# Order of the GpSimd work in a fused attention and routing kernel: where kept sums are weighed, where weight sums stand, and how group ends are cut

## The chip, the cores and the metric

The kernel runs on one core of one Trainium2 chip. The metric is device time in microseconds (us). A core has a matrix engine (PE, with its weight loads as PEld), a vector engine (DVE), a scalar engine (ACT), a general engine (POOL, GpSimd) and a sync engine (SP). Each takes its instructions strictly in the order of its own queue, and waits at the head of the queue until what an instruction needs is there. Almost all DMAs of this kernel are issued from SP's queue.

## What is computed

A polynomial-sketch attention gives x of 4352 rows and 128 columns; eight experts with a hidden layer of 1024 then work on x, each expert's output is multiplied by a routing weight per row (from a Sinkhorn iteration), and the eight are added:

```python
logits = x @ w_gate
P = np.exp(logits - logits.max())
for _ in range(8):
    P /= P.sum(1, keepdims=True) + 1e-09
    P /= P.sum(0, keepdims=True) + 1e-09
    P *= N / E
for e in range(E):
    h = np.maximum(x @ w1[e], 0.0)
    out += P[:, e:e + 1] * (h @ w2[e])
```

All is float32. The routing weights are positive, so x may be multiplied by the weight ahead of the first product: `relu(P x w1) w2` is `P (relu(x w1) w2)`. The kernel does so for most of the work.

## The kernel before

x is kept transposed, features on the partitions and 4352 rows of x as columns (`xT`). The expert work is cut into **groups** of columns (line 536 on) and, within a group, into **items**, one per expert. A step of an item is a first product (line 788: two halves of the output), its relu on ACT (line 792), additions on DVE that prepare a fast matrix multiplication in the manner of Strassen (two tiles at a time: lines 807 to 810; three tiles at a time: lines 841 and 861), and eight steps later the second products (line 931), which add up in four PSUM banks over all experts of the group. The second products use sums and differences of blocks of w2, which POOL makes once per expert (`sums_of_two`, lines 186 to 189; `sums_of_four`, line 225, ten instructions), stores to DRAM and later loads again (lines 182, 213).

Items 0 to 6 are unweighted: they run while the routing weights are still being computed (expert 0 on all columns, expert 1 on the first 1280), and their results stay in SBUF as **kept** sums. Items 7 to 46 are weighted. They form five groups of 3 x 256 columns (experts 1 to 7, or 2 to 7 in the group that starts at column 512), whose items have two blocks of eight steps, and a last group of 2 x 256 columns (experts 2 to 7), whose items have four blocks of four steps. For a weighted item, `prepare_x` loads the expert's routing weights, the same row on all partitions, from the DRAM tensor `pT` into a tile `xe` (line 562), and POOL multiplies x into it (line 574). Tiles `xe` and the weight tiles have two buffers each, so a load for an item waits until the item before the last is through with its buffer.

The kept sums must be weighed too before they are added at the group's end: `weigh_kept` loads weights into a tile `pb` (line 562; one buffer) and POOL multiplies them into the kept sums (line 585), and adds two such products where experts 0 and 1 were both kept (line 587). It is called when the second item of a weighted group starts.

At a group's end `part_of_twenty` combines the four banks in some 20 small operations, handed to DVE and ACT one per step (`at_leisure`), then adds the kept sums to all 768 columns at once, and `put` turns the result (line 598, DVE) and stores it with DMAs from SP (line 754): one per block of 32 features, twice as many where the columns cross one of the four batches of 34 blocks of 32 columns.

What sets the order: a planner (the Tile framework) places the instructions of every engine and queue. During the attention, and until the first weighted items, DVE and PE have the order in which the code names them. POOL and SP are free throughout, and in the rest of the weighted part all engines are: the planner takes an instruction when it estimates that its inputs and its buffer are ready, with program order as the rank. So an instruction that is named late can stand early in a queue. `keep_in_program_order(i)` ties `i` behind the instruction named just before it on the same engine or queue; it orders the issue and doesn't wait for the other to finish. Before, only four memsets have it (lines 465, 467).

The work is named in `steps`: at the start of item j it prepares weights and x of items j and j + 1, and then, in the group's second item, weighs the kept sums.

Of the kernel before, what the change touches and what calls it, by code (L numbers as in the profile page):

```python
# [10 lines left out]
F32 = mybir.dt.float32  # L11
U32 = mybir.dt.uint32
Act = mybir.ActivationFunctionType
Alu = mybir.AluOpType
# [36 lines left out]
def kernel(  # L51
# [12 lines left out]
    nc = tc.nc  # L64
    P = nc.NUM_PARTITIONS
# [63 lines left out]
    pT = dram.tile([E, N], F32, name="pT")  # L129
# [3 lines left out]
    for i in range(2):  # L133
        t = consts.tile([P, 2, 2, 2, D], F32, name=f"kvz{i}")
# [4 lines left out]
    for i in range(2):  # L139
        t = wk.tile([P, H + 1, NT + 1, D], F32, name=f"v{i}", bufs=1)  # L140
# [3 lines left out]
    loaded, pools = {}, []  # L144
# [64 lines left out]
    def sums_of_four(e, w2):  # L209

        ws = pools[0].tile([P, len(FORMS), FO // 4, H2], F32, tag="ws4", name="ws4")
        if e in stored_four:
            nc.sync.dma_start(out=ws, in_=stored_four[e])
            return ws

        def blocks(bs):
            b = w2[:, bs[0][1]::4, H2 * bs[0][0]:H2 * (bs[0][0] + 1)].unsqueeze(1)
            if len(bs) == 1:
                return b
            step = (bs[1][1] - bs[0][1]) * DM + (bs[1][0] - bs[0][0]) * H2  # L220
            return AP(tensor=b.tensor, offset=b.offset, ap=[b.ap[0], [step, 2], *b.ap[2:]])

        c = 0
        for ns, x, y, off in FOURS:
            nc.gpsimd.tensor_tensor(ws[:, c:c + len(ns)], blocks(x), blocks(y), op=Alu.subtract if off else Alu.add)  # L225
            c += len(ns)
        stored_four[e] = dram.tile([P, len(FORMS), FO // 4, H2], F32, name=f"ws4{e}")
        nc.sync.dma_start(out=stored_four[e], in_=ws)
        return ws
# [294 lines left out]
    NT3 = 256  # L524
# [33 lines left out]
                loaded_w[j] = *loaded_w[j][0:2], sums_of_four(e, loaded_w[j][1])  # L558

    def weights_of(e, lo, n, tag):  # L560
        pb = pools[0].tile([P, 3 * NT3], F32, tag=tag, name=tag, bufs=2 if tag == "xe" else 1)[:, 0:n]
        nc.sync.dma_start(out=pb, in_=pT[e:e + 1, lo:lo + n].to_broadcast([P, n]))
        return pb

    def prepare_x(j):
        g, e = items[j]
        lo, n, t, es, weighted = groups[g]
        x = xT[:, lo:lo + t * n]
        if not weighted:
            sources[j] = x  # L570
            return
        xe = weights_of(e, lo, t * n, "xe")
        for sl in (slice(0, 512), slice(512, 768)) if j == first_weighted else (slice(0, t * n),):
            nc.gpsimd.tensor_tensor(xe[:, sl], x[:, sl], xe[:, sl], op=Alu.mult)  # L574
        sources[j] = xe

    first_weighted = next(j for j, (g, e) in enumerate(items) if g == PLAIN)
# [1 line left out]
    def weigh_kept(g):  # L579

        lo, n, t, es, _ = groups[g]
        ys = []
        for e in range(es[0]):
            ys.append(kept[e][:, lo:lo + n * t])
            nc.gpsimd.tensor_tensor(ys[e], ys[e], weights_of(e, lo, n * t, "pb"), op=Alu.mult)  # L585
        for y in ys[1:]:
            nc.gpsimd.tensor_tensor(ys[0], ys[0], y, op=Alu.add)

    lower, upper = slice(0, H2), slice(H2, P)

    def at_leisure(do):

        soon.append(lambda: later.append(do))

    def put(y, lo, n, queues):
        b0, nb = lo // 32, n // 32
        yt = pools[0].tile([P, 3 * NT3 // 32, 32], F32, tag="yt", name="yt")[:, 0:nb, :]
        nc.vector.transpose(out=yt.rearrange("p b d -> p (b d)"), in_=y)
        store(yt, b0, b0 + nb, queues)

# [92 lines left out]
    def part_of_twenty(g, k):  # L693


        lo = groups[g][0]
        own = parts.setdefault(g, {})
        own[k] = room("zwmf"[k]).rearrange("p (s n) -> p s n", s=2)
        nc.scalar.copy(own[k].rearrange("p s n -> p (s n)"), sums[g][k])

        def do(out, a, b, off=False):
            at_leisure(lambda: nc.vector.tensor_tensor(out, a, b, op=Alu.subtract if off else Alu.add))  # L702

        if k == 0:
            own["y"] = pools[0].tile([P, 3, NT3], F32, tag="y", name="y")
            do(own["y"][:, 0], own[0][:, 0], own[0][:, 1])
        y = own["y"]
        if k == 1:
            do(y[:, 1], own[1][:, 0], own[0][:, 0], True)
        elif k == 2:  # L710
            do(y[upper, 2], own[2][upper, 0], own[0][upper, 0], True)
            do(y[lower, 2], own[2][lower, 0], own[0][lower, 1], True)
            do(y[lower, 2], y[lower, 2], own[2][lower, 1], True)
            do(y[lower, 1], y[lower, 1], own[1][lower, 1], True)
        elif k == 3:
            e0, e1, e2, e3 = (own[i] for i in range(4))
            t, c = (room(a).rearrange("p (s n) -> p s n", s=2) for a in "rx")
            d = e0[:, 1]

            def across(out, a):  # L720
                at_leisure(lambda: nc.scalar.copy(out, a))

            do(t[:, 0], e2[:, 1], e3[:, 0])
            do(t[:, 1], e1[:, 1], e3[:, 1], True)
            do(d[upper], t[upper, 1], e3[upper, 0], True)
            across(c[lower, 1], t[upper, 0])
            across(c[upper, 1], e3[lower, 0])
            do(t[upper, 1], d[upper], e2[upper, 1], True)
            do(t[lower, 1], t[lower, 0], t[lower, 1])
            across(d[lower], d[upper])  # L730
            across(c[lower, 0], t[upper, 1])
            across(c[upper, 0], t[lower, 1])
            do(e0[upper, 0], e1[upper, 1], e3[upper, 0], True)
            do(e0[upper, 0], e2[upper, 1], e0[upper, 0], True)
            do(y[upper, 1], y[upper, 1], e0[upper, 0])
            do(c[lower, 1], e3[lower, 0], c[lower, 1], True)
            do(y[:, 1], y[:, 1], c[:, 1], True)
            do(y[:, 0], y[:, 0], t[:, 1])
            do(y[:, 0], y[:, 0], c[:, 0])
            do(y[upper, 2], y[upper, 2], t[upper, 1], True)  # L740
            do(y[lower, 2], y[lower, 2], d[lower], True)
            flat = y.rearrange("p t n -> p (t n)")
            do(flat, flat, kept[0][:, lo:lo + 3 * NT3])
            at_leisure(lambda: put(flat, lo, 3 * NT3, (nc.sync,)))

    ends = (nc.scalar, nc.sync, nc.gpsimd, nc.scalar), (nc.sync, nc.scalar, nc.gpsimd, nc.sync)

# [190 lines left out]
    def steps():  # L938

        todo, sums_at, t = {}, {}, 0  # L940
        for k in range(len(blocks) + 2):
            if k == len(blocks):
                for i, ps in enumerate(last_products(k - 2)):
                    todo[t + i] = ps
            if k < len(blocks):
                j, q = blocks[k]
                g, e = items[j]
                lo, n, tiles, es, weighted = groups[g]
                if q == 0:
                    for i in (j, j + 1, j + 2 if j + 2 < first_weighted else j):  # L950
                        if i < len(items) and i not in loaded_w and (pools or i < first_weighted):
                            prepare_w(i)
                        if i < len(items) and i not in sources and (pools or i < first_weighted):
                            prepare_x(i)
                    if weighted and e == es[1]:
                        weigh_kept(g)
                m, step, sums_ = (four if tiles == 3 else two)(k)
                products = (twenty if tiles == 3 else seven)
            for c in range(m if k < len(blocks) else 4):
                if k < len(blocks):  # L960
                    step(c)
                for do in sums_at.pop(t, ()):
                    do()
                while soon:
                    soon.pop(0)()
                for b, p in todo.pop(t, ()):
                    second(b, p)
                if k < len(blocks) and c == 0:
                    for i in range(2, 10):
                        sums_at.setdefault(t + i, []).append(lambda i=i, f=sums_: f(i))  # L970
                    if k < len(blocks) - 2:
                        for i, ps in enumerate(products(k)):
                            todo.setdefault(t + LAG + i, []).extend((k, p) for p in ps)
                share = n / 480
                if k >= len(blocks):
                    while later:
                        later.pop(0)()
                elif later and (tiles == 3 or c % 2 or share > 0.9):
                    later.pop(0)()
                yield share  # L980
                t += 1
        while soon:
            soon.pop(0)()
        while later:
            later.pop(0)()
# [101 lines left out]
```

## Time and profile before

| | |
|---|---|
| time, median of 3 | 959.16 us (958.76 to 959.29) |
| profiled run | 958.96 us, span 957.2 us, mean granted PE clock 0.992 |
| first weighted matmul | 207.69 us |
| last matmul ends | 949.1 us |
| POOL, line 225 (sums of w2's blocks) | 70 instructions, 58.2 us |
| POOL, line 574 (weighted x) | 41 instructions, 74.0 us |
| POOL, line 585 (kept sums weighed) | 6 of 768 columns at 2016 ns, 2 of 512 at 1513 ns |
| DMAs of pb | 6 of 384 KB, 3.6 us to landing; 2 of 256 KB, 4.0 us |
| DMAs of xe | 34 of 384 KB, 4.6 us to landing; 6 of 256 KB, 4.7 us |
| DMAs of w1 and w2 | 82 of 512 KB, 4.7 us to landing (median) |

Busy time counts an engine's own work, not its waiting or the issue of DMAs. Matmuls are pipelined, so PE busy isn't PE at its peak. Idle time of an engine that isn't the bottleneck costs nothing by itself. In the chain that ended last, PE has 86% of the span, DMA, POOL and DVE 4% each.

### The profile page before, as it was taken

How to read it: one execution, taken by the hardware profiler on the slowest of the kernel's cores; microseconds unless marked ns; L12 is line 12 of the kernel's file. 1: busy time of each engine (PE TensorE's matmuls, PEld its weight loads, DVE VectorE, ACT ScalarE, POOL GpSimd, SP SyncE). 2: the span in 40 equal slices, each digit the busy share in tenths (PEclk: the TensorE clock that was granted, in tenths of full speed). 3: DMA queues.
4: the chain of work that ended last, by engine and by line, in shares of the span. 5: the costliest groups of instructions: out<-in, count | busy, mean ns of one | idle time of the engine just before them, and what ended most of it. 6: DMA issues, size and time to landing. Idle time of an engine off the chain costs nothing.

```text
span 957.2 us, 18202 instructions
## 1 busy us (share of the span) xinstructions
PE 929.7 (97%) x7162; PEld 514.4 (54%) x7162; DVE 697.0 (73%) x1195; ACT 419.7 (44%) x894; POOL 180.4 (19%) x177
## 2 busy tenths in 40 slices
PE   8999999999599999999999999999999999999996
PEld 6553535458355555555555555555555555555664
DVE  8787679999467779666786665976566976668555
ACT  2444345555144445444544444544444544445443
POOL 1000000274645621001010100010001232321010
PEclk9999999999799999999999999999999999999999
DMA  6600000232344353533453343444343555452640
GB/s 190 183 1 1 1 1 1 84 111 76 84 165 150 105 187 117 175 111 137 136 158 127 121 150 125 137 129 159 117 143 108 174 163 185 137 178 90 156 136 12
DMA packets 85221, 113.06 MB, mean 118 GB/s; under 512 B 22736, under 2 KB 66768, under 8 KB 80784
## 3 DMA queue, kind: packets, MB, share of 16 engines
q1 hardware_dynamic: 84112, 111.70, 36.8%
q8 instruction: 56, 0.92, 0.4%
q10 hardware_dynamic: 960, 0.13, 0.1%
q14 instruction: 29, 0.24, 0.1%
q0 software_dynamic: 64, 0.07, 0.0%
HBM read 99.03 MB, written 12.85 MB: 117 GB/s over the span
## 4 chain that ended last, share of the span: by engine, by line
PE 86%; DMA 4%; POOL 4%; DVE 4%; issue 1%; ACT 0%; SPq 0%; DVEq 0%; POOLq 0%; ACTq 0%
PE a L788 44%; PE s L931 37%; DMA pb<-pT 3%; POOL ws L225 2%; POOL kept L585 2%; PE a L354 1%; PE a L376 1%; PE a L323 1%; DMA qx<-in_q_dram 1%; POOL xe L574 0%; DMA pT<-lgT 0%; DVE y L702 0%; DMA v<-in_v_dram 0%; PE a L401 0%; PE a L292 0%
## 5 line engine op out<-in xcount | busy, mean ns | idle before, releaser
L788 PE MATMUL a<-xe,w 128*64 128x256 f32 (+1 forms) x2560 | 517.4, 471 | 10.8 <-POOL xe L574 10.8
L792 ACT ACTIVATE hb<-a 128x256 f32<-128x256 f32 (+3 forms) x384 | 189.2, 495 | 254.1 <-PE a L788 231.0
L792 ACT ACTIVATE hx<-a 128x256 f32<-128x256 f32 (+1 forms) x368 | 170.4, 463 | 232.2 <-PE a L788 207.4
L788 PEld LDWEIGHTS a<-xe,w 128*64 128x64 f32 x2560 | 198.1, 137 | 105.8 <-POOL xe L574 11.2
L931 PE MATMUL s<-hb,ws 128*64 128x256 f32 (+2 forms) x1312 | 234.8, 401 | 0.8 <-DVE hb L809 0.8
L841 DVE TENSOR_TENSOR hx<-hx 128x512 f32<-128x512 f32 (+1 forms) x204 | 152.0, 756 | 84.5 <-ACT hx L792 79.7
L931 PE MATMUL s<-hx,ws 128*64 128x256 f32 x1280 | 205.6, 379 | 0.2 <-DVE hx L809 0.2
L841 DVE TENSOR_TENSOR hb<-hb 128x512 f32<-128x512 f32 (+1 forms) x204 | 134.2, 667 | 97.5 <-ACT hb L792 93.5
L931 PEld LDWEIGHTS s<-hb,ws 128*64 128x64 f32 x1312 | 103.8, 137 | 118.5 <-issue 88.8
L574 POOL TENSOR_TENSOR xe<-xT,xe 128x768 f32<-128x768 f32 (+2 forms) x41 | 74.0, 1805 | 493.0 <-DMA xe<-pT 369.1
L931 PEld LDWEIGHTS s<-hx,ws 128*64 128x64 f32 x1280 | 101.9, 137 | 104.4 <-issue 73.6
L788 PE MATMUL a<-xT,w 128*64 128x480 f32 (+2 forms) x448 | 121.0, 506 | 1.3 <-DVE xT L395 1.2
L931 PE MATMUL s<-hb,w 128*64 128x256 f32 (+2 forms) x440 | 96.3, 426 | 1.1 <-DVE kept L622 1.0
L225 POOL TENSOR_TENSOR ws<-w 128x256 f32<-128x256 f32 (+1 forms) x70 | 58.2, 866 | 137.5 <-ACT hb L792 136.7
L931 PE MATMUL s<-hx,w 128*64 128x256 f32 x416 | 75.0, 379 | 0.8 <-DVE hx L810 0.8
L788 PEld LDWEIGHTS a<-xT,w 128*64 128x64 f32 x448 | 43.7, 137 | 33.5 <-issue 17.9
L931 PEld LDWEIGHTS s<-hb,w 128*64 128x64 f32 x440 | 38.4, 137 | 29.2 <-issue 11.1
L841 DVE TENSOR_TENSOR pqg<-hb 128x512 f32<-128x512 f32 x68 | 44.5, 696 | 0.0
L931 PEld LDWEIGHTS s<-hx,w 128*64 128x64 f32 x416 | 36.2, 137 | 14.8 <-DVE hx L810 1.2
L807 DVE TENSOR_TENSOR hb<-hb 128x960 f32<-128x960 f32 (+2 forms) x28 | 30.8, 1099 | 11.1 <-ACT hb L792 6.1
L807 DVE TENSOR_TENSOR hx<-hx 128x512 f32<-128x512 f32 x24 | 16.6, 691 | 28.4 <-ACT hx L792 28.3
L841 DVE TENSOR_TENSOR pqg<-hx 128x512 f32<-128x512 f32 x68 | 34.8, 551 | 0.0
(152 smaller groups left out, 538.7 us busy)
## 6 DMA issues: line engine op xcount, KB each, us to landing
w<-in_moe_w_dram SPq DMA_DIRECT2D x82, 512.0 KB, 4.7
ws<-ws SPq DMA_DIRECT2D x34, 1024.0 KB, 5.1
xe<-pT SPq DMA_DIRECT2D x34, 384.0 KB, 4.6
ws<-ws SPq DMA_DIRECT2D x12, 512.0 KB, 4.3
pb<-pT SPq DMA_DIRECT2D x6, 384.0 KB, 3.6
kx<-in_k_dram SPq DMA_DIRECT2D x4, 544.0 KB, 4.1
qx<-in_q_dram SPq DMA_DIRECT2D x4, 544.0 KB, 5.6
v<-in_v_dram SPq DMA_DIRECT2D x32, 64.0 KB, 4.6
```

The costliest lines, as they stand in the source:

```text
L225: nc.gpsimd.tensor_tensor(ws[:, c:c + len(ns)], blocks(x), blocks(y), op=Alu.subtract if off else Alu.add)
L323: nc.tensor.matmul(pv[64 * s:64 * (s + 1), i], kp[0:n, H * t + h].rearrange("p i j -> p (i j)"), vx[0:n, slots[h], t, :], start=(t == 0 an ...
L354: nc.tensor.matmul(banks[i][m][:, 0:n], wqf[sl, m, :], qT[sl, lo:hi], start=True, stop=True, tile_position=(64 * i, 0))
L376: nc.tensor.matmul(t[64 * i:64 * (i + 1), 0:n], kvz[:, (i + m) % 2, i].rearrange("p h d -> p (h d)"), ph[i][0][:, 0:n], start=True, stop=T ...
L574: nc.gpsimd.tensor_tensor(xe[:, sl], x[:, sl], xe[:, sl], op=Alu.mult)
L585: nc.gpsimd.tensor_tensor(ys[e], ys[e], weights_of(e, lo, n * t, "pb"), op=Alu.mult)
L788: nc.tensor.matmul(ph[sl], loaded_w[j][0][:, P * f + H2 * s:P * f + H2 * (s + 1)], sources[j][:, lo:hi], start=True, stop=True, tile_posit ...
L792: nc.scalar.activation(out=out, in_=ph, func=Act.Relu)
L807: nc.vector.tensor_tensor(ts[:, 0:2], h[:, 1::2], h[:, 0:2], op=Alu.subtract)
L841: nc.vector.tensor_tensor(out if not isinstance(out, tuple) else places(*out), places(*a), places(*b) if isinstance(b, tuple) else b, op=A ...
L931: nc.tensor.matmul(sums[g][i][H2 * s:H2 * (s + 1), n * place:n * (place + 1)], w, x, start=c == 1, stop=c == per, tile_position=(0, H2 * s))
```

## The change

There are four edits.

1. `weigh_kept` is called when a group's fourth item starts (`es[3]`), no longer its second. Its loads, products and additions are tied to program order.
2. The loads and products of the weighted x, and the ten instructions of `sums_of_four`, are tied to program order, and at an item's start `prepare_x` comes ahead of `prepare_w`.
3. `pb` has two buffers, like `xe` (the pool's number).
4. At the end of a group of three tiles the kept sums are added, and the result turned and stored, in three pieces of 256 columns; the tile `yt` is 256 columns wide with four buffers, before 768 with two.

```diff
         for ns, x, y, off in FOURS:
-            nc.gpsimd.tensor_tensor(ws[:, c:c + len(ns)], blocks(x), blocks(y), op=Alu.subtract if off else Alu.add)
+            tc.keep_in_program_order(nc.gpsimd.tensor_tensor(ws[:, c:c + len(ns)], blocks(x), blocks(y),
+                                                             op=Alu.subtract if off else Alu.add))
...
     def weights_of(e, lo, n, tag):
-        pb = pools[0].tile([P, 3 * NT3], F32, tag=tag, name=tag, bufs=2 if tag == "xe" else 1)[:, 0:n]
-        nc.sync.dma_start(out=pb, in_=pT[e:e + 1, lo:lo + n].to_broadcast([P, n]))
+        pb = pools[0].tile([P, 3 * NT3], F32, tag=tag, name=tag)[:, 0:n]
+        tc.keep_in_program_order(nc.sync.dma_start(out=pb, in_=pT[e:e + 1, lo:lo + n].to_broadcast([P, n])))
         return pb
+
+    def weigh(out, x, pb):
+        tc.keep_in_program_order(nc.gpsimd.tensor_tensor(out, x, pb, op=Alu.mult))
...
         for sl in (slice(0, 512), slice(512, 768)) if j == first_weighted else (slice(0, t * n),):
-            nc.gpsimd.tensor_tensor(xe[:, sl], x[:, sl], xe[:, sl], op=Alu.mult)
+            weigh(xe[:, sl], x[:, sl], xe[:, sl])
...
-            nc.gpsimd.tensor_tensor(ys[e], ys[e], weights_of(e, lo, n * t, "pb"), op=Alu.mult)
+            weigh(ys[e], ys[e], weights_of(e, lo, n * t, "pb"))
         for y in ys[1:]:
-            nc.gpsimd.tensor_tensor(ys[0], ys[0], y, op=Alu.add)
+            tc.keep_in_program_order(nc.gpsimd.tensor_tensor(ys[0], ys[0], y, op=Alu.add))
...
-        yt = pools[0].tile([P, 3 * NT3 // 32, 32], F32, tag="yt", name="yt")[:, 0:nb, :]
+        yt = pools[0].tile([P, NT3 // 32, 32], F32, tag="yt", name="yt", bufs=4)[:, 0:nb, :]
...
-            flat = y.rearrange("p t n -> p (t n)")
-            do(flat, flat, kept[0][:, lo:lo + 3 * NT3])
-            at_leisure(lambda: put(flat, lo, 3 * NT3, (nc.sync,)))
+            for i in range(3):
+                do(y[:, i], y[:, i], kept[0][:, lo + NT3 * i:lo + NT3 * (i + 1)])
+            for i in range(3):
+                at_leisure(lambda i=i: put(y[:, i], lo + NT3 * i, NT3, (nc.sync,)))
...
                     for i in (j, j + 1, j + 2 if j + 2 < first_weighted else j):
+                        if i < len(items) and i not in sources and (pools or i < first_weighted):
+                            prepare_x(i)
                         if i < len(items) and i not in loaded_w and (pools or i < first_weighted):
                             prepare_w(i)
-                        if i < len(items) and i not in sources and (pools or i < first_weighted):
-                            prepare_x(i)
-                    if weighted and e == es[1]:
+                    if weighted and e == es[3]:
                         weigh_kept(g)
```

## The prediction

> **What bounds the kernel now.** I read the page's busy table and its slices first, to see whether one engine is full and where it is not.
>
> ```profile
> PE 929.7 (97%) x7162; PEld 514.4 (54%) x7162; DVE 697.0 (73%) x1195; ACT 419.7 (44%) x894; POOL 180.4 (19%) x177
> PE   8999999999599999999999999999999999999996
> PEclk9999999999799999999999999999999999999999
> ```
>
> PE is the bound: 27.5 us of 957.2 are idle, and apart from the start and the end there is one hole, in the eleventh slice (239 to 263 us), where the clock digit falls too. Next, who PE waited for:
>
> ```profile
> PE a L788 <- POOL xe L574: 10.8, 1, 10.8
> PE s L931 <- DVE hx L810: 0.8, 1, 0.8
> PE s L931 <- DVE hb L809: 0.8, 1, 0.8
> ```
>
> One wait, for a weighted x made by POOL, is 10.8 us; the other two are under 1 us each. What did POOL do before it? Its timeline (start, length, what; in brackets the idle time before):
>
> ```profile
> 206.13 2.13 POOL L574 TENSOR_TENSOR xe<-xT,xe 128x768 f32<-128x768 f32 x1
> 211.94 1.82 POOL L585 TENSOR_TENSOR kept<-kept,pb 128x768 f32<-128x768 f32 x1 [3.69 <-DMA pb<-pT]
> ...
> 252.13 1.26 POOL L585 TENSOR_TENSOR kept<-kept,pb 128x512 f32<-128x512 f32 x1 [4.83 <-DMA pb<-pT]
> 253.47 1.26 POOL L587 TENSOR_TENSOR kept<-kept,kept 128x512 f32<-128x512 f32 x1
> 254.80 1.80 POOL L574 TENSOR_TENSOR xe<-xT,xe 128x768 f32<-128x768 f32 x1
> ```
>
> The weighing of the kept sums of all six groups (eight products, two additions) stands in one row between the x of item 8 and that of item 9. The tile pb has one buffer, so each load waits for the product before it. SP's queue shows the same row, and what stands behind it:
>
> ```profile
> 195.91 10.60 SPq L228 DMA_DIRECT2D ws<-ws  x2
> 206.56 41.09 SPq L562 DMA_DIRECT2D pb<-pT  x8
> 247.70 0.42 SPq L174 DMA_DIRECT2D w<-in_moe_w_dram  x1
> 248.17 0.42 SPq L562 DMA_DIRECT2D xe<-pT  x1
> ```
>
> Item 9's weights and x are issued only after the eighth pb, and POOL reaches its x at 254.80. The windows around the hole (length, PE, PEld, DVE, ACT, POOL busy, then the clock) give the after-effect:
>
> ```profile
> 245.80:256.70 10.90, 0.12 (x3) 0.05 (x2) 3.17 (x4) 0.12 (x1) 5.93 (x5) 0.68 0.58 156
> 256.70:258.70 2.00, 2.00 (x6) 0.71 (x8) 0.00 (x0) 0.00 (x0) 2.00 (x4) 0.50 0.00 0
> 258.70:261.00 2.30, 2.30 (x14) 1.02 (x12) 0.00 (x0) 0.88 (x2) 2.30 (x4) 0.74 0.00 0
> ```
>
> Last, DVE at the second of the small holes (883.1 to 885.2), where a group's end runs in pieces of 768 columns between the sums of the last group:
>
> ```profile
> 881.99 0.94 DVE L702 TENSOR_TENSOR y<-y,kept 128x768 f32<-128x768 f32 x1
> 882.86 0.41 DVE L809 TENSOR_TENSOR hx<-hx 128x256 f32<-128x256 f32 x1
> 883.19 0.96 DVE L598 STREAM_TRANSPOSE yt<-y 128x768 f32<-128x768 f32 x1
> 884.09 1.02 DVE L810 TENSOR_TENSOR hx<-hx 128x256 f32<-128x256 f32 x1
> ```
>
> PE waits for L809 (0.23 us) and L810 (0.76 us), each queued behind one of the wide pieces: 0.99 us.
>
> **What the Trainium skill says.** "TensorE: Matmul & The Clock Gate", Part 1: after about 3.4 us of idleness the clock drops to half, and comes back after about 3.4 us of work. The trace agrees: 0.50 for 2.0 us after the hole, 0.74 over the next 2.3, 1.00 from 261. "SBUF — State Buffer", Terms: DVE and GpSimd share one port pair, and the loser blocks for a whole instruction. The trace agrees: a 128x512 addition of line 807 took 2.30 us at 206.50, beside POOL's product (206.13 to 208.26), and 0.69 at 210.23. "DMA: Bandwidth & Descriptors", Anatomy of one DMA: the semaphore wait is made on the issuing sequencer, ahead of the transfer. The trace agrees: item 9's loads stand behind pb's waits on SP.
>
> **Price of the hole.** A three-tile item has 64 matmul records of line 788, so each 64th record starts an item. From there: item 7 starts at 207.69, 8 at 226.42, 9 at 256.65, 10 at 277.24, and 11 to 41 follow each other at 18.95 us with PE never idle. Items 8 and 9 took 30.23 + 20.59 = 50.82 us against 2 x 18.95 = 37.90: **12.9 us lost**, of which 10.8 is the wait and 1.6 the slow clock (2.0 x 0.50 + 2.3 x 0.26). The rest is the pipeline's refill.
>
> **The change, part by part.**
>
> *The weighing pinned into each group's fourth item.* It takes eight pb loads and 12.1 + 3.0 + 1.9 + 1.3 = 18.3 us of POOL work out of 206 to 254 and puts one or two products into items 10, 17, and so on. With that row gone the first items go like this, in times of the old trace. pT lands at about 185.8 and x of item 7 is loaded at 185.9; at 4.6 us (median of xe) it lands at 190.5, and two products of together 2.4 us end near 193. Ten sums of item 7 at 0.96 (16 took 15.33) end at 202.6; they are needed for its second products, 8 of 16 steps into the item: 207.7 + 9.5 = 217.2. SP stores them and loads x of item 8: ready near 210, needed at 226.4. Sums of item 8 end near 220, needed at 235.9. x of item 9 is loaded when item 7's first stage frees its buffer (226.4) and is ready near 233, against 245.4. Its w2 is free 7 or 8 steps into item 8 (about 235.9), lands about 4.7 later, and ten sums at 0.87 (8.6 us in the rows of items 10 to 13) end at 250, against 254.9. Every margin is positive, the least 4.6 us. Gain: 12.9.
>
> Where the weighing goes: for item 10, pb stands behind the store of item 11's sums on SP, which goes out about 5 us into item 11 (before: 282.18 with item 10 started at 277.24). Then 4.6 us of load, 2.0 of product, and x of item 12 at 1.9: ready about 13.5 us into item 11, against 18.95. What is queued behind: x and sums of item 12, which wait for w2 (lands near 14) anyway. In the later groups POOL has one product of 1.8 us per item, so 2 to 6 us more lie beside PE work. The last group's two loads and 4.1 us come in item 44, with two items left before use. Cost nothing, hidden behind those items' 18.95 (12.95) us of matmuls.
>
> *Sums behind the weighted x on POOL.* Same instructions, other order; it brings x forward by up to 8.6 us and sums back by 1.9, within the 4.6. Nothing by itself. In addition POOL's product of 206.13, which held the 2.30 us addition, moves to about 208.5. Behind that addition lies the first small wait, 0.76 us at 209.1. The new sums (210 to 220) may hold other additions: bounds 0.8 gained to 0.8 lost; I take **0.4 gained**.
>
> *A second pb buffer.* Two loads can go at once in the two groups that weigh two tiles. Nothing hangs on it after the move.
>
> *Ends in pieces of 256.* Per group 3 additions at 0.42 for one of 0.94, 3 transposes at 0.42 (128x256 in the tail) for one of 0.96: 0.6 us more of DVE, 3.1 in five groups, in stretches where DVE is busy 63 to 76% and PE loses nothing. Before the last group the narrow pieces let the sums pass earlier: up to 0.99 gained, or 0.6 lost by the extra work while DVE is full; I take **0.5 gained**. The stores: each piece issues 4 DMAs, or 8 where it crosses one of the b blocks of 34, so 72 instead of 32, 40 more x 0.48 us = 19 us of SP over 500 us, some 4 us per group. What waits behind them, x and w2 of a following item, has margins of 12 us: x is ready at 416.4 for item 18's start at 428.9. Four yt buffers hold three pieces, so no transpose waits for a store. Nothing.
>
> Sum: 12.9 + 0.5 + 0.4 = 13.8 off the profiled span of 957.2. That run's time was 958.96 and the median of the runs 959.16, both about 2 us above the span, so 959.16 - 13.8 = **945.4 us**.
>
> **The rivals.**
> - *A part of the hole comes back elsewhere.* For it: DVE is busy 18.6, 17.8 and 19.5 us of 20 between 180 and 240, and the sums now hold the port pair there; the tightest margin is 4.6 us. Against it: DVE waits again by 243.95, so its backlog was gone, and POOL's load between 206 and 250 is about 22 us against 19. A new wait of some 4 us with 1.6 of slow clock leaves a gain of 8: 951.
> - *SP's queue blocks x (the slower side).* Weight loads aren't pinned. If the planner puts w2 of the next item ahead of its x on SP, x waits until mid-item: about 8 us later. In items 9 to 13 x is now ready 3.7 us before its need (292.53 against 296.20), so from a delay of 3.7 us on it decides: (8 - 3.7 + 1.6) x 5 = 30 lost, less 13.8: 975. Against it: x is traced ahead of w2, and before it stood ahead of it in all these items.
> - *The weighing isn't moved.* Were the pins not to hold, 959 would stay; but nearly all late POOL work is pinned in one chain, the additions too.
> - *More than the sum.* All PE idleness and slow clock from 186 us to the last matmul is 14.7, which gives 944.5; less than 943.5 would need a shorter tail, and no edit touches it.
>
> **How the numbers follow.** Forecast 0.68 (943.5 to 947.5), partial gain 0.20 (947.5 to 956), unmoved 0.03, slower 0.06, more 0.03. The range 943.5 to 952 takes in the bounds of the two small terms and most of the partial case. A change under 0.2% (1.9 us) can't be told from none: faster 0.91, same 0.03, slower 0.06.
>
> **What would show it.** PE's wait for POOL xe gone, items 8 and 9 at 18.95 us and the clock at 1.00 in 240 to 265; the pb loads one or two per group, the first near 287; the 0.8 us waits smaller; the tail after the last matmul still about 8 us. I am wrong if a wait for ws, hx or xe of over 2 us appears between 207 and 340, or if the items after 353 take longer than 18.95.

## The result and the profile after

The changed kernel took 947.31 us (median of four runs, 946.85 to 948.05) against 959.13 us before: a ratio of 0.9878, 95% interval 0.9861 to 0.9895, so 11.8 us less. The forecast was 945.4 us, 13.8 less. The profiled run has a span of 945.5 us. The sum of the working is nearly right, but two of its terms are clearly off, in opposite directions.

From the page of the kernel after, the busy table and its slices:

```profile
PE 928.3 (98%) x7162; PEld 548.7 (58%) x7162; DVE 699.2 (74%) x1215; ACT 419.2 (44%) x894; POOL 192.5 (20%) x177
PE   8999999999999999999999999999999999999996
PEclk9999999999999999999999999999999999999998
```

The hole in the eleventh slice is gone, and the fallen clock behind it too. The window of the hole, before and then after (length, PE, PEld, DVE, ACT, POOL busy, clock, DMA share, GB/s):

```profile
240.00:265.00 25.00, 14.22 (x94) 8.53 (x92) 10.25 (x15) 4.91 (x10) 14.53 (x15) 0.80 0.34 100
240.00:265.00 25.00, 25.00 (x192) 16.26 (x190) 17.72 (x24) 10.21 (x21) 15.30 (x17) 1.00 0.32 101
```

Over the whole span PE worked about as long as before (928.3 against 929.7 us): the time came out of its idleness. POOL and SP, in the stretch that held the row of eight products (start, length, what; in brackets the idle time before and what ended it):

```profile
206.35 1.92 POOL L567 TENSOR_TENSOR xe<-xT,xe 128x768 f32<-128x768 f32 x1 [5.68 <-DMA xe<-pT]
208.23 8.27 POOL L225 TENSOR_TENSOR ws<-w 128x256 f32<-128x256 f32 x10
230.02 1.98 POOL L567 TENSOR_TENSOR xe<-xT,xe 128x768 f32<-128x768 f32 x1 [13.51 <-DMA xe<-pT]
240.65 8.42 POOL L225 TENSOR_TENSOR ws<-w 128x256 f32<-128x256 f32 x10 [8.65 <-PE a L793]
...
295.20 1.81 POOL L567 TENSOR_TENSOR kept<-kept,pb 128x768 f32<-128x768 f32 x1 [6.15 <-DMA pb<-pT]
297.62 1.95 POOL L567 TENSOR_TENSOR xe<-xT,xe 128x768 f32<-128x768 f32 x1 [0.61 <-DMA xe<-pT]
```

```profile
289.07 0.33 SPq L229 DMA_DIRECT2D ws<-ws  x1
289.45 0.42 SPq L563 DMA_DIRECT2D pb<-pT  x1
289.97 0.86 SPq L563 DMA_DIRECT2D xe<-pT  x1
```

The first block is POOL's, the second SP's. x of item 9 is ready at 232.0 and its item starts at 245.12; the working had said 233 and 245.4. The first pb is issued at 289.45, right behind the store of item 11's sums; the working had said near 287. The start of the last group on DVE, where the wide pieces stood:

```profile
868.91 0.41 DVE L706 TENSOR_TENSOR y<-y,kept 128x256 f32<-128x256 f32 x1
869.25 0.41 DVE L814 TENSOR_TENSOR hx<-hx 128x256 f32<-128x256 f32 x1
869.58 0.41 DVE L706 TENSOR_TENSOR y<-y,kept 128x256 f32<-128x256 f32 x1
869.92 0.41 DVE L815 TENSOR_TENSOR hx<-hx 128x256 f32<-128x256 f32 x1
```

The narrow additions alternate with the sums, and PE no longer waits for either sum here. Last, the waits at the end (engine, line, for whom: total us, times, longest), where there is something new:

```profile
ACT w L675 <- POOL kept L591: 3.9, 1, 3.9
...
PE a L793 <- ACT hx L797: 1.3, 1, 1.3
```

Line 675 is a copy of weighed kept sums that belongs to the very last group end (`last_part`, `w[lower] = k2[lower]`). It stands in ACT's queue where item 45 starts (904.80):

```profile
904.19 0.38 ACT L797 ACTIVATE hx<-a 128x256 f32<-128x256 f32 x1 [0.47 <-PE a L793]
908.51 0.40 ACT L675 COPY w<-kept 64x256 f32<-64x256 f32 x1 [3.94 <-POOL kept L591]
908.82 1.57 ACT L797 ACTIVATE hx<-a 128x256 f32<-128x256 f32 x5
```

While ACT waits 3.94 us for POOL, no relu runs, the banks of the first products aren't emptied, and PE stops for 1.33 and then 0.40 us. (Item 45 takes 2.53 us longer than before; what makes up the other 0.8 isn't shown.)

The starts of the items (every 64th record of the first product on xe), before and after, show where the time went:

| | before | after | gained so far |
|---|---|---|---|
| item 8 starts | 226.42 | 226.17 | 0.25 |
| item 10 starts | 277.24 | 264.07 | 13.17 |
| item 42 starts | 879.04 | 865.95 | 13.09 |
| item 43 starts | 893.43 | 878.90 | 14.53 |
| item 45 starts | 919.33 | 904.80 | 14.53 |
| item 46 starts | 932.28 | 920.28 | 12.00 |
| last matmul ends | 949.07 | 937.07 | 12.00 |
| span | 957.2 | 945.5 | 11.7 |

So: 12.92 in the hole, 1.44 at the start of the last group, 2.53 lost again in item 45 (15.47 us instead of 12.95), 0.3 lost in the tail, where the stores are issued as long after the last matmul as before (3.55 us) and take longer. The 0.25 by item 8 can't be told from chance: in a second profile of the same kernel, further below, item 8 starts at 227.04.

### The profile page after: what moved, and what is told of

It reads as the page before. It is cut to its first block, busy times and chain, and to the rows that moved or that the text cites. A ratio compares the mean times of both kernels' runs of the same rounds, so it can differ in the third digit from the quotient of the medians.

```text
span 945.5 us, 18262 instructions
## 1 busy us (share of the span) xinstructions
PE 928.3 (98%) x7162; PEld 548.7 (58%) x7162; DVE 699.2 (74%) x1215; ACT 419.2 (44%) x894; POOL 192.5 (20%) x177
## 4 chain that ended last, share of the span: by engine, by line
PE 92%; DVE 4%; DMA 1%; issue 1%; POOL 0%; ACT 0%; SPq 0%; DVEq 0%; POOLq 0%; ACTq 0%
PE a L793 48%; PE s L936 41%; PE a L355 1%; PE a L377 1%; PE a L324 1%; DMA pb<-pT 1%; DMA kx<-in_k_dram 0%; DVE hb L814 0%; DVE hx L846 0%; DVE hb L812 0%; PE a L293 0%; DVE kp L309 0%; DVE qa L367 0%; DVE kT L280 0%; DVE qT L275 0%
## 5 line engine op out<-in xcount | busy, mean ns | idle before, releaser
L793 PEld LDWEIGHTS a<-xe,w 128*64 128x64 f32 x2560 | 208.9, 137 | 77.4 <-ACT hx L797 1.8
L846 DVE TENSOR_TENSOR hb<-hb 128x512 f32<-128x512 f32 (+1 forms) x204 | 131.0, 652 | 101.6 <-ACT hb L797 97.3
L567 POOL TENSOR_TENSOR xe<-xT,xe 128x768 f32<-128x768 f32 (+2 forms) x41 | 84.3, 2058 | 570.2 <-DMA xe<-pT 415.8
L936 PEld LDWEIGHTS s<-hb,ws 128*64 128x64 f32 x1312 | 108.9, 137 | 112.6 <-issue 85.3
L936 PEld LDWEIGHTS s<-hx,ws 128*64 128x64 f32 x1280 | 106.1, 137 | 98.6 <-issue 72.6
L225 POOL TENSOR_TENSOR ws<-w 128x256 f32<-128x256 f32 (+1 forms) x70 | 60.0, 892 | 13.5 <-PE a L793 11.7
L846 DVE TENSOR_TENSOR pqg<-hb 128x512 f32<-128x512 f32 x68 | 50.8, 787 | 0.0
L812 DVE TENSOR_TENSOR hb<-hb 128x960 f32<-128x960 f32 (+2 forms) x28 | 28.7, 1027 | 12.9 <-PE s L936 7.0
```

The costliest lines, as they stand in the source:

```text
L225: tc.keep_in_program_order(nc.gpsimd.tensor_tensor(ws[:, c:c + len(ns)], blocks(x), blocks(y), op=Alu.subtract if off else Alu.add))
L567: tc.keep_in_program_order(nc.gpsimd.tensor_tensor(out, x, pb, op=Alu.mult))
L793: nc.tensor.matmul(ph[sl], loaded_w[j][0][:, P * f + H2 * s:P * f + H2 * (s + 1)], sources[j][:, lo:hi], start=True, stop=True, tile_posit ...
L812: nc.vector.tensor_tensor(ts[:, 0:2], h[:, 1::2], h[:, 0:2], op=Alu.subtract)
L846: nc.vector.tensor_tensor(out if not isinstance(out, tuple) else places(*out), places(*a), places(*b) if isinstance(b, tuple) else b, op=A ...
L936: nc.tensor.matmul(sums[g][i][H2 * s:H2 * (s + 1), n * place:n * (place + 1)], w, x, start=c == 1, stop=c == per, tile_position=(0, H2 * s))
```

## The experiments

**Is it the place, the tie, or the buffer?** Three kernels each make one part of the change alone, and a fourth adds the pieces. They ran on one chip, with the kernel before at 959.08 us. Their profiles, like all below, are of one run each.

The place alone:

```diff
-                    if weighted and e == es[1]:
+                    if weighted and e == es[3]:
```

> The kernel before with the weighing called in the fourth item instead of the second, nothing tied. Theory A (it is the tie to program order, or the buffer, that decides, since a free planner places the eight products where it thinks pb is ready): the row stays ahead of item 9's x, the wait of 10.8 us too; 959.1 us. Theory B (the place in the code decides): the wait goes, 946 us.

958.47 us, ratio 0.9994 (0.9985 to 1.0002): no difference. The order on POOL is that of before, and PE waited 9.55 us for item 9's x:

```profile
PE a L788 <- POOL xe L574: 9.5, 1, 9.5
```

Where the call stands in the code changes nothing here while the planner is free. Theory B falls.

The tie alone, for the weighing only:

```diff
-            nc.gpsimd.tensor_tensor(ys[e], ys[e], weights_of(e, lo, n * t, "pb"), op=Alu.mult)
+            pb = weights_of(e, lo, n * t, "pb", True)
+            tc.keep_in_program_order(nc.gpsimd.tensor_tensor(ys[e], ys[e], pb, op=Alu.mult))
         for y in ys[1:]:
-            nc.gpsimd.tensor_tensor(ys[0], ys[0], y, op=Alu.add)
+            tc.keep_in_program_order(nc.gpsimd.tensor_tensor(ys[0], ys[0], y, op=Alu.add))
```

(and the load of pb tied likewise).

> The kernel before with only the weighing's loads, products and additions tied to program order (second item, one pb buffer). Theory A: the wait for xe of 10.8 us and the slow clock go (-12.9). The copy of the weighed kept sums on ACT, which the planner puts right behind the last group's weighing, now waits in item 42 as it does in item 44 of the changed kernel (+2.5): 948.7 us. Theory B (the tie alone isn't enough): 959. A rival on the copy (it waits only because the weighing stands in the fourth item): 946.2 us.

948.86 us, ratio 0.9893 (0.9876 to 0.9909). Items 8 and 9 take 18.95 us each, with the weighing in the second item and one buffer: the tie alone fills the hole, and brings 10.2 us of the 11.8 of the whole change. The copy on ACT does wait, here where item 43 starts (881.81), with PE idle for 1.06 us behind it:

```profile
884.45 0.40 ACT L674 COPY w<-kept 64x256 f32<-64x256 f32 x1 [3.71 <-POOL kept L590]
```

So the copy's wait isn't a matter of the fourth item.

One word alone, the second buffer:

```diff
-        pb = pools[0].tile([P, 3 * NT3], F32, tag=tag, name=tag, bufs=2 if tag == "xe" else 1)[:, 0:n]
+        pb = pools[0].tile([P, 3 * NT3], F32, tag=tag, name=tag)[:, 0:n]
```

> The kernel before with one word changed: pb has two buffers. The eight products stay in one row ahead of item 9's x. Theory C (the row costs PE something only because each load waits for the product before it): a pair of loads takes about 6.2 us where two took 10.8, the row ends near 236 instead of 254.7, x of item 9 is ready near 238, ahead of its start at 245.4: no wait for xe, 946.2 us. Theory A in its strict form (the row must leave this place): a wait of 4 us or more stays, 953 to 959 us.

953.93 us, ratio 0.9939 (0.9916 to 0.9962), with runs from 949.96 to 955.33; the profile is of the slowest. Neither theory holds as it stands: the time lies in theory A's range, but not for A's reason. The row ends at 236.9, x of item 9 is ready at 239.1, and PE doesn't wait for it, as theory C said. But PE waits for DVE instead. From the waits of this kernel between 207 and 250 us:

```profile
PE s L931 <- DVE hb L841: 3.1, 1, 3.1
PE s L931 <- DVE hx L841: 1.1, 1, 1.1
PE s L931 <- DVE hb L809: 0.8, 1, 0.8
PE s L931 <- DVE kept L622: 0.4, 1, 0.4
```

DVE has no idle time there, and the reason stands in its timeline: additions that take 0.4 to 0.7 us elsewhere take 2.0 to 2.3 us beside POOL's products.

```profile
221.00 2.04 DVE L841 TENSOR_TENSOR pqg<-hx 128x256 f32<-128x256 f32 x1
222.96 2.30 DVE L841 TENSOR_TENSOR hx<-hx 128x512 f32<-128x512 f32 x1
...
228.07 2.04 DVE L619 TENSOR_TENSOR kept<-z,f 128x256 f32<-128x256 f32 x1
```

The pieces on top of the two buffers:

```diff
-            do(flat, flat, kept[0][:, lo:lo + 3 * NT3])
-            at_leisure(lambda: put(flat, lo, 3 * NT3, (nc.sync,)))
+            for i in range(3):
+                do(y[:, i], y[:, i], kept[0][:, lo + NT3 * i:lo + NT3 * (i + 1)])
+            for i in range(3):
+                at_leisure(lambda i=i: put(y[:, i], lo + NT3 * i, NT3, (nc.sync,)))
```

> Two pb buffers and the group ends in pieces of 256 columns, nothing tied or moved. Against the run with two buffers alone it shows the pieces: if the 0.99 us wait at the start of the last group and its refill come from the wide pieces, 1.4 us less, 944.8 us, with no copy of kept sums waiting on ACT, since the weighing is long done. If the gain of 1.4 us there came from another part of the change: 946.2 us.

949.72 us, ratio 0.99 (0.9886 to 0.9915). The waits for DVE between 209 and 241 are there again (4.9 us in sum, with the 0.8 of before). The last group's item 42 takes 12.95 us, against 14.39 in the run with two buffers alone: 1.44 us, just what the changed kernel gains there. The pieces are that gain. The other 3 us between the two profiles lie in item 8 (22.22 against 25.34 us), ahead of any end of a weighted group: its longest wait was 1.5 us here and 3.1 there, and the clock stayed at 1.00 here.

**What holds DVE up: POOL's products, or the loads?** The same kernel as the one with two buffers, with the same loads and the same order of POOL and SP, but kept sums weighed over 32 columns only (the rest of the weighing is left out):

```diff
-            nc.gpsimd.tensor_tensor(ys[e], ys[e], weights_of(e, lo, n * t, "pb"), op=Alu.mult)
+            pb = weights_of(e, lo, n * t, "pb")
+            nc.gpsimd.tensor_tensor(ys[e][:, 0:32], ys[e][:, 0:32], pb[:, 0:32], op=Alu.mult)
...
-            nc.gpsimd.tensor_tensor(ys[0], ys[0], y, op=Alu.add)
+            nc.gpsimd.tensor_tensor(ys[0][:, 0:32], ys[0][:, 0:32], y[:, 0:32], op=Alu.add)
```

> The kernel before with two pb buffers, and the kept sums weighed and added over 32 of their columns only; the rest of that weighing is left out. All eight loads stay, and the order of every queue is that of the run with two buffers (span 953.5 us), where PE waited 0.4 to 3.1 us at a time for DVE between 209 and 240. Theory D (POOL's long products hold the port pair, DVE's additions take 2 us instead of 0.7 and fall behind): those waits go but for the 0.76 us at 209, items 8 and 9 take 18.95 us, 946.2 us. If the loads of pb or the order cost PE the time: 951 to 954 us.

946.78 us, ratio 0.9869 (0.9855 to 0.9884), on a chip where the kernel before took 959.30. Items 8 and 9 take 18.95 us each, and in that stretch PE waits for DVE once, the 0.8 us of before. The windows (length, then PE, PEld, DVE, ACT, POOL busy with their instructions, clock, DMA share, GB/s), first with two buffers:

```profile
220.00:230.00 10.00, 8.86 (x68) 4.57 (x66) 9.94 (x8) 3.33 (x7) 8.74 (x5) 1.00 0.30 108
```

then with the short products, and last the kernel before, with one buffer:

```profile
220.00:230.00 10.00, 10.00 (x77) 8.36 (x75) 8.22 (x17) 4.28 (x9) 3.42 (x7) 1.00 0.51 158
220.00:230.00 10.00, 10.00 (x81) 8.58 (x78) 9.77 (x13) 4.15 (x9) 5.24 (x3) 1.00 0.23 79
```

With POOL busy for 8.74 of 10 us DVE gets 8 instructions done, with 3.42 it gets 17, though the DMAs move more. It is POOL's products, not the loads, as theory D said. Whether their length or their sum decides isn't separated: the cut makes both smaller. With one buffer the products, spaced by their loads, keep POOL busy for 5.24 us; DVE gets 13 instructions done and PE doesn't wait for it, but the row ends too late for x.

**The changed kernel with parts taken back.** One chip, the kernel before at 958.66 us.

The weighing untied again, x and sums still tied:

```diff
-            weigh(ys[e], ys[e], weights_of(e, lo, n * t, "pb"))
+            nc.gpsimd.tensor_tensor(ys[e], ys[e], weights_of(e, lo, n * t, "pb", False), op=Alu.mult)
```

> The changed kernel with the weighing's loads, products and additions untied (x and the sums stay tied). The planner puts two products ahead of item 8's x and six ahead of item 9's, with two buffers. Theory C: the row ends near 236, x of item 9 is ready near 238 and PE doesn't wait for it; the copy on ACT has nothing to wait for; 944.8 us, less than the changed kernel. Theory A in its strict form: the hole comes back, 950 to 957 us.

951.55 us, ratio 0.9923 (0.9906 to 0.9941). Again neither: the time lies in theory A's range, but the hole isn't back. PE has no wait for x, but six waits for DVE, 0.3 to 1.6 us each and 5.7 in sum, between 205 and 241. The copy on ACT costs nothing here, since the weighing is long done. The kernel below with the copy tied, which differs from this one in the tied weighing, took 945.62 us on the same chip: with the copy out of the way, tying the weighing is worth 5.9 us.

The old order of preparation, all ties kept:

```diff
-                        if i < len(items) and i not in sources and (pools or i < first_weighted):
-                            prepare_x(i)
                         if i < len(items) and i not in loaded_w and (pools or i < first_weighted):
                             prepare_w(i)
+                        if i < len(items) and i not in sources and (pools or i < first_weighted):
+                            prepare_x(i)
```

> The changed kernel with the weights prepared ahead of x at an item's start, as before; all ties stay. My prediction gave the order of x and sums nothing by itself. If the ties make the order count: x of an item stands behind its sums on POOL, and on SP behind their store, and these wait for w2, which is free only in the middle of the item before. Item 9 then starts some 11 us late and each of items 10 to 13 takes about 29.6 us instead of 18.95: with the slow clock +50 to +65, 1000 to 1012 us. If the order doesn't count: 947.3 us.

1055.62 us, ratio 1.102 (1.0967 to 1.1074): slower than before by a tenth. Items 9 to 13 start 30.6 to 31.3 us after each other, 1 to 2 us more than expected. From the waits of this kernel over its whole span:

```profile
PE a L793 <- POOL xe L567: 78.8, 22, 9.7
```

On SP the load of x now stands behind the load of w2, which is free only in the middle of an item, and in the first group also behind the store of the sums made from it (for item 9: w2 at 235.94, the store at 248.30, x at 248.67). I had expected this to cost something only where POOL makes the sums, up to item 13. It goes on, in smaller portions: item 46 starts 103 us later than in the changed kernel, 59 of them up to item 14. SP ahead of item 36 shows why (stores of a group end went before, for 3.3 us):

```profile
824.97 0.39 SPq L213 DMA_DIRECT2D ws<-ws  x1
825.45 0.40 SPq L175 DMA_DIRECT2D w<-in_moe_w_dram  x1
825.91 0.57 SPq L563 DMA_DIRECT2D xe<-pT  x1
```

That is 12.7 us into item 35 (813.23); behind the landing stand, on POOL, four sums for the last group and then x, ready at 838.03, where the item should have begun at 832.2. So with the ties the order of x and weights is worth over 100 us; without ties, in the kernel before, the planner had put x ahead of w2 by itself.

**The copy on ACT.** In the changed kernel, the last group alone weighed in its second item:

```diff
-                    if weighted and e == es[3]:
+                    if weighted and e == es[1 if tiles == 2 else 3]:
```

> The changed kernel, but the last group's kept sums are weighed in its second item; the other groups keep the fourth. Theory P (the planner puts ACT's copy of the weighed sums wherever it takes the weighing to be done, and that is too early on the chip): the copy moves along, waits some 4 us near the end of item 42, and the 2.5 us stay lost, 947.3 us. Theory Q (the fourth item is too late for the copy's own need): the wait goes, 944.8 us.

948.74 us, ratio 0.9902 (0.9887 to 0.9917): no gain. The copy moved along, to 879.4, and waited there:

```profile
878.99 0.38 ACT L797 ACTIVATE hx<-a 128x256 f32<-128x256 f32 x1 [0.47 <-PE a L793]
884.07 0.40 ACT L675 COPY w<-kept 64x256 f32<-64x256 f32 x1 [4.69 <-POOL kept L591]
```

Item 43 takes 16.61 us instead of 12.95. Theory Q falls, and P fits: the planner places the copy earlier than the sums are ready on the chip, wherever the weighing stands. In the changed kernel pb's load went out at 899.25, 7.4 us into item 44, right behind a load of sums (898.88) on SP.

The place left, the copy tied:

```diff
-            nc.scalar.copy(w[lower], k2[lower])
+            tc.keep_in_program_order(nc.scalar.copy(w[lower], k2[lower]))
```

> The changed kernel with one tie more: ACT's copy of the weighed kept sums stays in program order, behind the last relu of the last group. The weighing keeps its place in item 44. Theory P: PE's wait for hx in item 45 goes, item 45 takes 12.95 us instead of 15.47, 944.8 us. If PE lost the 2.5 us to POOL's products on the port pair that DVE shares, or to the loads of pb: 947.3 us.

945.62 us, ratio 0.9868 (0.9853 to 0.9883). Item 45 takes 13.20 us. In this run item 18 took 19.76 us, with PE waiting 0.55 for DVE. Both kernels once more on one chip, with the kernel before at 959.30:

> The changed kernel unaltered, on the same chip as the others: 947.3 us.

> The changed kernel with ACT's copy tied, once more, on the same chip as the changed kernel: 945.6 us, 1.7 to 2.5 us below it if the copy was the cause of the wait in item 45; no difference if the earlier run was chance.

The changed kernel took 948.21 us (947.96 to 948.44), with the copy tied 945.17 (944.55 to 945.90), ratios 0.9884 (0.9870 to 0.9899) and 0.9852 (0.9835 to 0.9868). The four runs of one and of the other don't overlap: 3.0 us. The changed kernel's item 45 took 15.34 us this time, the other's 13.17, with the copy behind the last relu and no wait in front of it:

```profile
932.40 0.41 ACT L675 COPY w<-kept 64x256 f32<-64x256 f32 x1
```

With the copy tied, and in the two groups that weigh two tiles one product per item:

```diff
-                    if weighted and e == es[3]:
-                        weigh_kept(g)
+                    at = (e - es[0]) - (3 if tiles == 3 else 2)
+                    if weighted and 0 <= at < es[0]:
+                        weigh_kept(g, at)
```

> The changed kernel with ACT's copy tied, and in the two groups that weigh two tiles one product per item (the second and the addition an item later; in the last group from its third item on). In the run with the tied copy alone item 18 took 19.76 us instead of 18.95, with POOL's two products and addition in a row. If that row holds up DVE: 18.95, and 0.8 us less than the tied copy alone, 944.8 us. If not: the same as it, 945.6 us.

944.75 us (944.35 to 945.01), ratio 0.9848 (0.9833 to 0.9863). Items 9 to 41 start 18.95 us apart without exception, 43 to 46 12.95; after 218 us no wait of PE is longer than 0.2 us until the end. It is below both kernels of the case, but can't be told from the tied copy alone (their runs overlap, and item 18 lost only 0.13 us in that kernel's second run). That POOL's row in item 17 held DVE up is thus only argued.

## Why the prediction was right, and where not

- **The price of the hole** (12.9) came out at 12.92, and the clock stayed at 1.00, as the working said. The path of the first items agrees with the trace to 3.5 us (the sums of item 8 end at 216.5, put near 220). The least margin was put at 4.6; the working's own figures, 250 against 254.9, give 4.9, and the trace 5.5 (sums of item 9 ready at 249.1).
- **The weighing at its new places, "cost nothing", with "two items left before use"**: this step failed, for the last group. It cost 2.53 us. I had taken the use to be the group's end. But the copy of line 675 is free for the planner, which placed it in ACT's queue ahead of the time at which the sums were weighed, and everything behind it on ACT waited. The profile of before had it: its copy (line 671) ran at 875.78, 70 us ahead of the rest of that group end, with no wait for POOL, since the weighing was done by 254.7. I had asked who waits behind pb and behind POOL, and not where the readers of the weighed sums stand. The runs with the copy moved and with it tied show it. Of the working's two signs of being wrong, a wait of over 2 us between 207 and 340 didn't come; a lengthened item after 353 did, item 45, with 15.47 us for 12.95. That the point of the forecast came within 2 us is in part luck: this loss and the gain from the pieces, both missed, partly cancel.
- **Ends in pieces, 0.5 gained**: 1.44. The mechanism was right and the size off: I bounded the gain by PE's idle 0.99 us. The items' starts held the whole price (14.38 against 12.95 in the steady state, 1.43), just as I had read them for the hole. And "0.6 lost by the extra work" wasn't seen.
- **The small wait at 209, 0.4 gained**: the wait of 0.76 us is gone, but one of 0.52 stands at 217 instead, so 0.2 was gained, and not by the step that I gave. The product that I had moved to 208.5 stands at 206.35 and holds an addition of DVE as before (1.93 us, 0.43 elsewhere), at the line below; why no wait followed at 209 isn't shown.

```profile
206.63 1.93 DVE L814 TENSOR_TENSOR hb<-hb 128x256 f32<-128x256 f32 x1
```

- **The order of x and sums, "nothing by itself"**: wrong as part of this change; without ties no run has tried it. With the ties it is what keeps x ahead of w2 on SP. My slower rival (x behind w2 on SP) had the mechanism and half the price: in the first group about 12 us were lost per item where I had put 6, since x then stands behind the making and storing of the sums too. I gave it 0.06 since the diff names x first, and that is indeed why it didn't come.
- **A part of the hole comes back elsewhere (0.20), by the sums holding the port pair**: not in the changed kernel, but it is what happens when the row stays and stands dense: with two buffers 4.7 us of new waits, and items 7 and 8 take 8.7 us longer in all, slow clock included (21.09 against 18.73, 25.34 against 18.95), in the slowest of four runs; with the pieces added, and no slow clock, 5.65 (21.11 and 22.22). The rival had put 5.6.
- **A second pb buffer, "nothing hangs on it after the move"**: not tried in the changed kernel; with the weighing tied, one buffer is enough to fill the hole. Where the row stays, the buffer alone takes the wait for x away.

The Trainium skill's "SBUF — State Buffer", Terms, has the loser of the port pair blocked for a whole instruction: the additions of 2.0 to 2.3 us beside POOL's products of about 2 us agree. The run with short products shows that these products hold DVE up; that they do it through the ports is the page's account, which no run here separates from another. Its "TensorE: Matmul & The Clock Gate", Part 1, names about 3.4 us of idleness before the clock falls; here the 3.11 us wait of the two-buffer kernel was enough: the clock was 0.50 from 240 to 245 us, as it was after 10.8.

## What to carry to other kernels

Where a planner places instructions, moving a call in the code may move nothing, and tying one instruction can delay it past the place where its readers were put: list every reader of what you delay, on every engine, and look in the trace where each stands now. A tie to program order makes the written order count, so the order has to be right first: the load that is free soonest goes ahead. Price a hole by the distance between the starts of equal pieces of work, which includes refill and slow clock, and not by the idle time alone.

## What the runs showed of the hardware

I had taken a denser row of POOL work to be cheaper, since it ends sooner. Here it wasn't: eight products of 1.6 to 2.1 us and two additions, ended 18 us sooner, cost PE 4.7 us more in waits for DVE between 218 and 240 in the profiled run, as DVE's additions beside them take up to 2.3 us instead of 0.7. Cut to 32 columns, the same row of eight loads and products costs PE no wait that the kernel before doesn't have.
